# Gated linear attention and a GELU feed-forward on one core: the third unit's decay logits are loaded ahead of w_in, w_in comes in pieces of 512, 1024 and 512 columns, and the planner's priorities are drawn anew

## The chip, the cores and the metric

One core of a Trainium2 chip runs the whole program. The metric is the device time in microseconds (us). The kernel before takes 182.77 us (median of three runs, 182.22 to 183.18). The profiled execution has a span of 181.1 us from its first to its last recorded instruction, in a run of 183.18 us.

## What is computed

```python
def _attn_ref(q, k, v, f_logit):            # each 4 x 8 heads x 768 steps x 48
    f = 1.0 / (1.0 + np.exp(-f_logit))
    state = 0                                # per head 48 x 48
    for t in range(S):
        state = f[t][:, None] * state + outer(k[t], v[t])
        y[t] = q[t] @ state
x = y with the heads side by side            # 3072 tokens x 384
h = x @ w_in                                 # 384 x 2048
out = (0.5 * h * (1 + erf(h / sqrt(2)))) @ w_out     # 2048 x 384
```

The recurrence is computed in chunks of 128 steps. Inside a chunk it becomes matrix products of keys and queries that are scaled by exponentials of summed log decays; a 48 x 48 state per head is carried from chunk to chunk.

## The kernel before, in words

**Units and groups.** The 3072 tokens are 24 chunks of 128. Two chunks make a unit (12 units, numbered from 0); each unit's tokens are also one group of the feed-forward. Units 0 to 4 are "pair" units: each of their inputs comes in one transfer of 384 KB (line 449). Later units load each chunk by itself (line 457, 192 KB).

**Names of the operations** (given in the code as `name=`; the number behind is that of the unit, chunk or group):
- E and L (ScalarE, lines 494 and 497): exponential and logarithm of a unit's logits `fl`, 0.84 us each. C (TensorE, lines 526 and 515): sums of the log decays. RG, GT, GL (ScalarE, lines 543, 549, 570): exponentials of the sums. In units 2 to 4 the second chunk's sums come from G, a subtraction on VectorE (line 535).
- KP and QP (VectorE, for chunks 2 and 3 one each on GpSimd, line 576): keys and queries times these exponentials. VC (line 583): values cast to bf16, on GpSimd except in unit 1.
- Tk and Tq (TensorE, line 611): transposes of KP and QP in units 0 to 3; KQ (line 617) moves them to `kq`. From unit 4 on the transposes are DMAs (line 599).
- A (TensorE, line 784 in pair units): scores; AM (VectorE, line 631): masked scores. S (line 806): the chunk's contribution to the state; R, T, SB (VectorE line 655, GpSimd lines 657 and 662): the carried state. YI and YX (lines 826 and 705): outputs from the scores and from the state. YB (line 675), XT (line 691) and X (line 694): the outputs, transposed, as the group's input `xT`.
- F1 (TensorE, line 875): eight blocks per group, named F1.group.block, six matmuls each: `xT` times 256 columns of `w_in`. Blocks 0 and 1 take theirs from the first 512 columns of `w_in`, blocks 2 and 3 from the next 512, and so on. GE (ScalarE, line 885): the exact GELU of one block. F2 (line 896): four blocks of four matmuls per chunk, block r with piece r of `w_out`. O and st: eviction and store.

GE needs another activation table than E, L, RG, GT and GL; a change of table is a load of 1.28 us on ScalarE (line 953). F1 and F2 have four PSUM banks between them, so a fifth F1 waits for the GELU of the first.

**The order.** [...] That order is made when the program is built, by a planner (`Plan.run`, line 116): it places the ready operation with the earliest start by assumed durations, and breaks ties by a priority. To the priorities of each stretch of 20 it adds random numbers, whose seeds and spread stand in `SEEDS` (line 28). Where the planner sees TensorE idle in the first 30 us it inserts junk matmuls (line 947) that keep the engine busy.

**The transfers.** `LOADS` (line 238) lists them in order: `f0` is the logits of unit 0, `k`, `v`, `q` its keys, values and queries, `i` a piece of `w_in` and `o` a piece of `w_out`. The inputs go out from SyncE on the hardware DMA queue (q1 in the profile). The weights must be cast from f32 to bf16, so GpSimd issues them on the software queue (q0), in GpSimd's own program order, between its arithmetic. Both queues run on the same 16 DMA engines. The planner treats them as one chain, one transfer after another. On the chip only this much of the chain is kept, by `load` (line 382): a transfer whose predecessor in the list is on the other queue waits for one earlier transfer of that other queue.

```python
gate = None
if i and order[i - 1][0] != eng:
    back = 4 if eng == "pool" else 2
    for j in range(i - back, -1, -1):
        if order[j][0] != eng:
            gate = order[j][1]
            break
```

Before, this gives: `i0` waits for `f1`; `k2` waits for nothing of the other queue; `i1` waits for `k2`; `i2` and the pieces of `w_out` follow `i1` without a wait; `f3` waits for `o3`.

## Time and profile before

| | busy us | share of the span |
|---|---|---|
| TensorE matmul | 171.7 | 95% |
| of it junk matmuls (line 947, 36 of them) | 10.4 | 6% |
| ScalarE | 125.2 | 69% |
| VectorE | 96.3 | 53% |
| GpSimd | 53.6 | 30% |

A busy TensorE is not the same as a useful one: the junk matmuls are all in the first 28 us and stand for waiting. The part of the profile to read for this change is therefore the opening, in which the engine waits for inputs and weights. The stretches of the trace (busy time in windows), the answer on DMA (packets of each queue in a window) and the chain of waits show it. "To landing" of a transfer is the time from the start of its issue to its completion.

### The profile page before, as it was taken

How to read it: one execution, taken by the hardware profiler on the slowest of the kernel's cores; microseconds unless marked ns; L12 is line 12 of the kernel's file. 1: busy time of each engine (PE TensorE's matmuls, PEld its weight loads, DVE VectorE, ACT ScalarE, POOL GpSimd, SP SyncE). 2: the span in 40 equal slices, each digit the busy share in tenths (PEclk: the TensorE clock that was granted, in tenths of full speed). 3: DMA queues.
4: the chain of work that ended last, by engine and by line, in shares of the span. 5: the costliest groups of instructions: out<-in, count | busy, mean ns of one | idle time of the engine just before them, and what ended most of it. 6: DMA issues, size and time to landing. Idle time of an engine off the chain costs nothing.

```text
span 181.1 us, 4916 instructions
## 1 busy us (share of the span) xinstructions
PE 171.7 (95%) x1990; PEld 132.3 (73%) x1990; DVE 96.3 (53%) x194; ACT 125.2 (69%) x212; POOL 53.6 (30%) x116
## 2 busy tenths in 40 slices
PE   7788889999999999988999999999999999999993
PEld 2356669966787688785779689976697986886972
DVE  5289750058898564244896692527691625362110
ACT  2775198963899189999967759777585578560720
POOL 7657870003043641140176113112435110300000
PEclk9999999999999999999999999999999999999999
DMA  6999999949997898999999999999999872814102
GB/s 148 261 261 226 268 170 203 200 115 267 278 266 142 186 197 170 249 227 171 216 179 213 215 175 207 195 187 189 185 245 181 181 162 47 166 37 91 43 0 87
DMA packets 106998, 32.61 MB, mean 180 GB/s; under 512 B 102113, under 2 KB 106081, under 8 KB 106977
## 3 DMA queue, kind: packets, MB, share of 16 engines
q1 hardware_dynamic: 105056, 29.07, 79.7%
q0 software_dynamic: 1776, 3.15, 9.8%
q8 instruction: 15, 0.25, 0.6%
q10 hardware_dynamic: 144, 0.10, 0.2%
q14 instruction: 7, 0.05, 0.1%
HBM read 25.17 MB, written 4.72 MB: 165 GB/s over the span
## 4 chain that ended last, share of the span: by engine, by line
PE 64%; ACT 15%; DMA 15%; SPq 3%; issue 1%; DVE 0%; DVEq 0%
PE ps L875 26%; PE ps L896 25%; ACT gT L885 7%; DMA fl<-in_f_logit_dram 7%; DMA win<-in_moe_w_in_dram 5%; ACT L953 4%; SPq L449 3%; DMA kq<-sc 2%; PE ps L722 2%; PE ps L758 2%; PE ps L917 1%; ACT gt L549 1%; PE ps L521 1%; PE ps L699 1%; PE ps L745 1%
## 5 line engine op out<-in xcount | busy, mean ns | idle before, releaser
L885 ACT ACTIVATE gT<-ps 128x512 bf16<-128x512 f32 x96 | 57.5, 671 | 24.6 <-PE ps L875 23.0
L875 PE MATMUL ps<-xT,win 128*128 128x256 bf16 x576 | 68.7, 273 | 1.3 <-ACT gT L885 0.9
L896 PE MATMUL ps<-wout,gT 128*128 128x384 bf16 x368 | 66.0, 326 | 0.0
L875 PEld LDWEIGHTS <-win 128*128 128x128 bf16 x576 | 61.6, 114 | 3.9 <-issue 1.2
L896 PEld LDWEIGHTS <-gT 128*128 128x128 bf16 x368 | 34.2, 98 | 19.5
L583 POOL CAST vb<-vt 128x384 bf16<-128x384 f32 x22 | 12.6, 584 | 52.5 <-DMA vt<-in_v_dram 52.4
L631 DVE TENSOR_TENSOR am<-ps,mask 128x512 bf16<-128x512 f32 x28 | 17.6, 684 | 15.1 <-PE ps L722 15.1
L901 DVE COPY osb<-ps 128x384 f32<-128x384 f32 x20 | 11.1, 556 | 25.9 <-PE ps L896 18.2
L657 POOL TENSOR_TENSOR tn<-rr,gl 128x384 f32<-128x384 f32 x16 | 14.0, 872 | 35.2 <-DVE rr L655 34.6
L576 DVE TENSOR_TENSOR sc<-qt,gt 128x384 bf16<-128x384 f32 x23 | 14.0, 616 | 13.7 <-ACT gt L549 13.7
L576 DVE TENSOR_TENSOR sc<-kt,rg 128x384 bf16<-128x384 f32 x23 | 13.5, 597 | 11.3 <-ACT rg L543 11.3
L953 ACT ACT_TABLE_LOAD x15 | 19.2, 1283 | 0.3
L662 POOL CAST sb<-tn 48x192 bf16<-48x192 f32 x40 | 14.8, 371 | 11.6 <-DVE tn L651 6.6
L494 ACT ACTIVATE fl<-fl 128x768 f32<-128x768 f32 x12 | 10.1, 842 | 10.5 <-DMA fl<-in_f_logit_dram 10.5
L675 DVE CAST yb<-ps 128x384 bf16<-128x384 f32 x22 | 11.9, 555 | 7.4 <-PE ps L758 3.7
L631 DVE TENSOR_TENSOR am<-ps,maskp 128x512 bf16<-128x512 f32 x20 | 12.5, 684 | 2.2 <-PE ps L784 1.4
L543 ACT ACTIVATE rg<-ps 128x384 f32<-128x384 f32 x21 | 10.3, 503 | 4.4 <-PE ps L523 2.8
L549 ACT ACTIVATE gt<-ps 128x384 f32<-128x384 f32 x21 | 10.2, 503 | 3.9 <-PE ps L523 3.3
L947 PE MATMUL ps<-junk 128*128 128x512 bf16 (+3 forms) x36 | 10.4, 423 | 2.1 <-POOL junk L939 1.3
L655 DVE TENSOR_TENSOR rr<-ps,tn 128x384 f32<-128x384 f32 x16 | 8.9, 553 | 3.5 <-POOL tn L657 1.8
L497 ACT ACTIVATE lf<-fl 128x768 bf16<-128x768 f32 x12 | 10.1, 843 | 0.4
L947 PEld LDWEIGHTS <-junk 128*128 128x128 bf16 x36 | 3.6, 111 | 6.2 <-issue 3.5
(74 smaller groups left out, 130.4 us busy)
## 6 DMA issues: line engine op xcount, KB each, us to landing
out_dram<-osb SPq DMA_DIRECT2D x19, 192.0 KB, 3.1
fl<-in_f_logit_dram SPq DMA_DIRECT2D x14, 192.0 KB, 3.8
kt<-in_k_dram SPq DMA_DIRECT2D x14, 192.0 KB, 3.8
qt<-in_q_dram SPq DMA_DIRECT2D x14, 192.0 KB, 3.7
vt<-in_v_dram SPq DMA_DIRECT2D x14, 192.0 KB, 3.9
fl<-in_f_logit_dram SPq DMA_DIRECT2D x5, 384.0 KB, 6.2
kt<-in_k_dram SPq DMA_DIRECT2D x5, 384.0 KB, 6.2
vt<-in_v_dram SPq DMA_DIRECT2D x5, 384.0 KB, 5.7
```

What stands on the lines that cost most here:

```text
L549: P.add("ACT", 0.40, lambda g=gps[j], gtv=gtv: nc.scalar.activation(gtv(), g.t()[:, 0:HD].rearrange("q (p h d) -> q p h d", h=2, d=D), AF. ...
L576: P.add("POOL" if pl else "DVE", 0.80 if pl else 0.475, lambda a=a, y=y, j=j, w=w, pl=pl, b=(gtv if w else rg): (nc.gpsimd if pl else nc.v ...
L583: P.add("ACT" if hv else "POOL", 0.40 if hv else 0.47, lambda y=y, j=j, hv=hv: (nc.scalar.copy if hv else nc.gpsimd.tensor_copy)(y["vb"].t ...
L631: P.add("POOL" if pl else "DVE", 1.15 if pl else 0.61, lambda hh=hh, pl=pl: (nc.gpsimd if pl else nc.vector).tensor_tensor(ams[hh].t(), ap ...
L657: P.add("POOL", 0.83, lambda: nc.gpsimd.tensor_tensor(tn.t(), rr.t(), glb(), ALU.mult), rd=[("rr", n), ("gl", n)], wr=[("tn", n)], bufs=[r ...
L662: P.add("POOL", 0.36, lambda hh=hh: nc.gpsimd.tensor_copy(sb.t()[64 * hh:64 * hh + D, :, D * hh:D * hh + D], tn.t()[64 * hh:64 * hh + D, : ...
L675: P.add("ACT" if help_ else "DVE", 0.40 if help_ else 0.475, lambda: copier(help_)(yb.t()[:, i, :], yp.t()[:, 0:HD]), rd=[("yp", n)], wr=[ ...
L875: nc.tensor.matmul(hps.t()[:, i * tok:(i + 1) * tok].rearrange("a (s t) -> a s t", s=s), col(fo)[:, kk, :], xT.t()[:, :, kk, :], start=(kk ...
L885: nc.scalar.activation(to, fr, AF.Gelu)
L896: nc.tensor.matmul(op.t()[:, 0:d_model], gT.t()[:, fo, s_ * C:(s_ + 1) * C], wout[fo // 4][:, fo % 4, :], start=(fo == 0), stop=(fo == FO ...
L947: nc.tensor.matmul(o.opens.t()[:, 0:w], junk[:, 0:C], junk[:, 0:w], start=True, stop=True, skip_group_check=True)
L953: nc.scalar.preload_act_table_set({"exp": "natural_log_exp_and_others", "gelu": "gelu_and_others"}[o.table])
```

## The change

It does three things. The logits of unit 2 (`f2`) are loaded before the first pieces of `w_in`, so that ScalarE can do that unit's exponentials early, before its first change to the GELU table. The first piece of `w_in` is made smaller, so that the first F1 blocks can start on less data, and the larger second piece follows it at once. The first unit's queries move ahead of its keys and values. The random priorities of nine of the twelve stretches are drawn with other seeds, which makes another order on every engine.

```diff
-SEEDS = [1643, 41, 3215, 1275, 2533, 2502, 823, 887, 1264, 763, 2447, 3095]
+SEEDS = [1131, 1014, 2287, 2045, 3867, 2749, 2245, 1296, 1264, 763, 2447, 126]
...
-WIN = [1024, 512, 512]
+WIN = [512, 1024, 512]
...
-LOADS = ['f0', 'k0', 'v0', 'q0', 'f1', 'v1', 'k1', 'q1', 'i0', 'k2', 'f2', 'v2', 'q2', 'i1', 'i2', 'i3', 'o0', 'o1', 'o3', 'o2', 'f3', 'k3', 'q3', 'u4', 'v3']
+LOADS = ['f0', 'q0', 'k0', 'v0', 'f1', 'v1', 'k1', 'q1', 'f2', 'i0', 'i1', 'k2', 'v2', 'q2', 'i2', 'i3', 'o0', 'o1', 'o3', 'o2', 'f3', 'k3', 'q3', 'u4', 'v3']
```

(`i3` names no piece and loads nothing.) In the built program the rule of `load` now gives other waits: `i0` waits for `v1`; `i1` follows it without one; `k2` waits for `i0`; `i2` waits for `f2`; `o0` and `o1` follow `i2` without a wait; `f3` waits for `o3` as before.

The order of the built program around the opening, on TensorE: A1, F1.0.0, C of unit 2, F1.0.1, YI1, YX of unit 1, XT, F1.0.2, XT, F1.0.3, F1.0.4, Tk of chunk 4, F1, Tk of chunk 5, F1, S2, F1, Tq of chunk 4, F1, Tq of chunk 5, two F1, A2. Before it was: A1, three F1, YI1, YX, F1, XT twice, C of unit 2, twelve F1, six F2, and only then Tk and Tq of chunk 4. There are 25 junk matmuls instead of 36; no other instruction of TensorE is added or removed.

On GpSimd: VC twice, one SB, `i0`, `i1`, the second SB, KP2, T, SB twice, QP3, T, `i2`, `o0`, `o1`, SB twice, T, SB twice, VC of unit 2 twice, T, `o3`, SB twice, `o2`. On ScalarE the exponentials RG, GT and GL of unit 2 now stand before the first GELU, where before they stood behind the sixteenth.

## The prediction

> **What bounds the kernel now.** First the busy times and the slices of the page.

> ```profile
> PE 171.7 (95%) x1990; PEld 132.3 (73%) x1990; DVE 96.3 (53%) x194; ACT 125.2 (69%) x212; POOL 53.6 (30%) x116
> ...
> DMA  6999999949997898999999999999999872814102
> ```

> TensorE sets the end. Of its 171.7 us, 10.4 are junk, so 161.3 are useful. The timeline of TensorE shows it without a gap worth naming after 27.35 (0.44 at 55.05, 0.45 at 79.20, 0.4 at 84.14, some 1.5 us in all), and 3.0 us follow its end at 178.1. Useful work before 27.35 is therefore 161.3 - (150.75 - 1.5) = 12.0 us: 15.3 us of the opening are lost, and only there can much be won. The second line shows the DMA engines full in just that time.

> The chain of waits, in order of time, says what the opening waits for:

> ```profile
> 4.38 6.17 DMA fl<-in_f_logit_dram
> ...
> 10.84 9.78 DMA win<-in_moe_w_in_dram
> ...
> 20.67 2.16 PE ps L875 x18
> ...
> 26.38 1.13 PE ps L947 x5
> 27.52 1.32 PE ps L875 x12
> ```

> F1 starts at 20.67, when `i0` lands; junk at 26.38 waits for the first GELU, which stands behind E and L of unit 2. Their logits are late (ScalarE's timeline, idle 3.89 us before E):

> ```profile
> 22.56 0.84 ACT L494 ACTIVATE fl<-fl 128x768 f32<-128x768 f32 x1 [3.89 <-DMA fl<-in_f_logit_dram]
> ```

> Now the DMA answer (packets, MB, share of 16 engines), one us at a time. From 13 to 14 us, before `w_in` flows:

> ```profile
> q1 hardware_dynamic: 684, 0.26, 128.5%
> ```

> From 15 to 16 us, while `i0` flows:

> ```profile
> q0 software_dynamic: 86, 0.18, 92.5%
> q1 hardware_dynamic: 87, 0.03, 19.0%
> ```

> This is the line that decides. The two queues get packet for packet. A packet of `w_in` is 2 KB, one of the inputs 384 bytes, so the inputs fall from 684 packets a us to 87. It lasts from 14.5 to 19.1; `k2`, issued at 10.32, takes 10.7 us instead of the 6.2 of its forerunners.

> [...]

> **The change, part by part.**

> *Queries first, junk, seeds.* QP0 can start at 7.3 instead of 7.75; the four multiplies then end 0.4 us earlier, and A0 comes 0.7 earlier. This gain ends in the wait for `w_in` and is worth nothing. Eleven junk matmuls less cost and win nothing: they ran in waits. The seeds permute the same work; after 27.35 they can win at most the 1.5 us of gaps. I take 0, with -1 to +1.

> *`f2` earlier.* The first eight loads are through at about 14.0 (8,259 packets of 1,024 a load). `f2` is ninth now: done at 14.0 + 957/690 = 15.4, landing at about 16.5 instead of 22.5. E and L follow KQ on ScalarE (until 18.3) and end at 20.0. Five exponentials (0.37 each, GL 0.1) and G follow, then the table load, so the first GELU runs at about 25, 0.6 earlier.

> *`i0` smaller, but behind `v1`.* `v1` lands at 5.87 + 6.2 = 12.1; `i0` is issued at 12.2 instead of 10.84. From issue to first data took 3.7 us for `i0` (full queue) and 2.4 for `i1` (23.7 - 21.33). I take 3.7: data from 15.9, after `f2`. 384 packets at the 150 a us of 25 to 26 us take 2.5; completion 1.4 later, as before (19.2 to 20.63). It lands at 19.8 (18.5 to 20.5). F1.0.0 starts behind A1 at 19.9: 0.8 earlier. `i1` flows next, 384 packets at about 86: until 22.7, landing 24.3.

> *`k2` behind `i0`.* The new wait. Queued behind it on SyncE are `v2` and `q2`, and for these KP4, KP5, QP4, QP5, VC and, in order on TensorE, everything from Tk4 on. Issue at 19.8, first data 1.5 later, as with `f3` (issued 37.75; 548 packets by 40 at 690 a us): 21.3. The software queue then holds 125 packets of `i1`, 384 of `i2` and 128 each of `o0` and `o1` (393 KB at 3 KB), which GpSimd has issued by about 21: `i2` waits only for `f2`, not for `k2`. Before, `i1` waited for `k2` (21.0) and flowed from 23.7; in the gap `f2`, `v2` and `q2` came at full rate. Now there is no gap. Packet for packet, 765 software packets pass before most of `k2`'s 1,024: 125/86 = 1.4 us, 384/113 = 3.4 (113 is the rate of 24 to 25 us), and 0.79 MB at the 0.21 MB a us of 30 to 34, stretched by 15% = 4.3. Sum 9.1: at 30.4 `k2` has 260 packets left, 0.4 us more. It lands at 31.9, `v2` and `q2` 1.5 us apart at 33.4 and 34.9.

> *TensorE with this.* F1.0.0 to 20.6, C2 to 21.1, F1.0.1 to 21.7; YI1 waits for VectorE (QP3 on GpSimd ends at about 18.1 and Tq at 18.35; then KQ 0.68, R 0.55 and four AM of 0.62: 22.1), YX to 23.3; YB to 24.4; F1.0.2 with `i1` at 24.5, three F1 and two XT (0.655 and 0.17 each): 26.8. There it stands at Tk4, with one F1 (0.655) more done than the kernel before at 27.35: a lead of 27.35 + 0.65 - 26.8 = 1.2 us. KP4 takes 0.55 after `k2`: Tk4 at 32.5. The wait costs 5.7; S2 waits 0.2 for VC (0.95 after `v2`), Tq5 0.2 for QP5. Net 5.7 + 0.4 - 1.2 = **4.9 us**.

> *After that.* `o3` stands on GpSimd behind VC of unit 2, so it is issued at about 36.5 instead of 25.4. Alone it needs 2.4 + 2.0 + 1.4: 42.3. `f3` waits for it:

> ```profile
> SPq L449 <- DMA wout<-in_moe_w_out_dram: 16.8, 1, 16.8
> ```

> That wait ended at 37.75 before; 4.6 us later now, in step with TensorE, which has F1 and F2 of two groups to do. No further cost, and nothing catches up later with TensorE full. 182.8 + 4.9 = 187.7.

> **The rivals.**

> *Faster: inputs and weights don't hinder each other much.* Then `k2` lands at 21.3 + 1.5 + 1.1 = 23.9, `q2` at 26.9; no wait at Tk4, and the lead of 1.2 stays: 181.6. For it: the 7.1 MB in question would be through by 29.5 at 261 GB/s. Against it: 87 packets against 684, four us long.

> *Equal time instead of equal packets.* 3.0 us a load: `k2` 25.4, `v2` 28.4, `q2` 31.4. S2 waits 1.2 us, Tq4 1.4: 182.8 + 2.6 - 1.2 = 184.2. Against it, the shares of 92.5 and 19.0%.

> *The clock falls as well.* [...] Against it: part of that work waits for `q2` anyway.

> *`i0` flows early* (2.4 us after issue, at 14.6) and catches `f2`, which then lands at about 23. C2 blocks TensorE till 24.8, but SyncE's `k2` runs in the gap, since `i2` waits for `f2`; `q2` is again the last, at 35. About 187.5, with the stall elsewhere.

> **How the numbers follow.** Main case and early `i0`, which end alike: 0.55. Half clock 0.20. Equal time 0.10. Faster 0.15, of which 0.03 for a lead eaten by new gaps (no change); 0.02 of the equal-time case falls there too. So faster 0.12, same 0.05, slower 0.83. The range takes the main case with the seeds' 1 us and `i0`'s landing, equal time at its lower end and half clock at its upper: 184.0 to 190.0. It leaves out the faster case.

> **What would show it.** `f2` landing near 16.5 and F1 at 19.9 show the first steps right. The packets of q1 between 22 and 30 us, about 60 to 110 a us beside q0, and `k2` landing near 32, show the decisive one; TensorE must be idle from about 27 to 32 before line 611, then `f3` must go out near 42. If `k2` lands before 27, the forecast is wrong. After 60 us the traces should run in parallel.

## The result, and the profile after

The changed kernel takes 187.43 us (median of four runs, 186.54 to 188.09) against 182.5 for the kernel before on the same chip: a ratio of 1.026 (95% interval 1.021 to 1.031), 4.9 us more. The profiled execution spans 184.7 us, in a run of 186.54; before, it was 181.1, in a run of 183.18. So the two traces are only 3.6 us apart: one is of the fastest of four executions, the other of the slowest of four. What makes up the other 1.3 us of the 4.9 stands in no trace. In three of the experiments below, one execution of four took over 1.5% longer than the fastest; the ratios leave it out, the medians do not.

The page's row of TensorE, its granted clock and the DMA engines in 40 slices of 4.6 us:

```profile
PE 174.6 (95%) x1979; PEld 132.4 (72%) x1979; DVE 100.1 (54%) x194; ACT 126.4 (68%) x212; POOL 53.8 (29%) x116
...
PEclk9999589999999999999999999999999999999999
DMA  6999998199993999998989989979999793926102
```

The granted clock before:

```profile
PEclk9999999999999999999999999999999999999999
```

The junk is less (8.9 us instead of 10.4) and the engine is busier by 2.9. Part of that is the clock, which is halved from 17.6 to 24.4 us (mostly in the fifth and sixth slices); it was full before. The DMA row has a new hole, in the slice from 32 us on.

The longest pieces of the chain of waits from 5 to 36 us (start, length, what):

```profile
5.69 6.31 DMA vt<-in_v_dram
12.30 6.85 DMA win<-in_moe_w_in_dram
20.20 12.56 DMA qt<-in_q_dram
34.73 1.31 PE ps L875 x12
```

No E, no GELU and no `w_in` of 1024 columns ends last any more. `v1` releases `i0`, `i0` releases the inputs of unit 2, and the last of these, `q2`, takes 12.6 us. It then stops VectorE (QP4), and QP4 stops TensorE (Tq of chunk 4): from A1 to this Tq (20.85 to 33.40 us) TensorE starts its operations in the order in which the program was built. The timelines of VectorE and of TensorE:

```profile
32.78 0.56 DVE L576 TENSOR_TENSOR sc<-qt,gt 128x384 bf16<-128x384 f32 x1 [3.16 <-DMA qt<-in_q_dram]
```

```profile
20.85 1.07 PE L784 MATMUL ps<-kq 64*64 64x128 bf16 x32
21.85 0.29 PE L947 MATMUL ps<-junk 128*128 128x128 bf16 x1
21.93 1.49 PE L875 MATMUL ps<-xT,win 128*128 128x256 bf16 x6
...
28.89 0.82 PE L875 MATMUL ps<-xT,win 128*128 128x256 bf16 x6 [0.56 <-ACT gT L885]
29.54 0.39 PE L611 MATMUL ps<-ident,sc 128*128 128x128 bf16 x4
...
33.40 0.40 PE L611 MATMUL ps<-ident,sc 128*128 128x128 bf16 x4 [0.72 <-DVE sc L576]
```

A1 starts at 20.85 and the first F1 at 21.93, where the forecast has 19.9 for F1 and, by its sum, about 19.1 for A1. Tk4, which was to stand for 5.7 us, starts at 29.54 with no wait before it.

Why `q2` is slow, from the answers on DMA (packets, MB, share of 16 engines). From 22 to 23 us:

```profile
q1 hardware_dynamic: 732, 0.28, 107.0%
q0 software_dynamic: 4, 0.01, 3.4%
```

and from 27 to 28 us:

```profile
q0 software_dynamic: 77, 0.19, 99.2%
q1 hardware_dynamic: 73, 0.03, 14.9%
```

The inputs first have the engines to themselves. From 27 to 28 us they get one packet for each packet of the weights. Before that they get fewer still, from 25 to 26 us:

```profile
q0 software_dynamic: 154, 0.18, 111.9%
q1 hardware_dynamic: 9, 0.00, 2.0%
```

The issue of `q2` was over by then (20.20 to 22.89). Why the turns are not even in this stretch is not shown. So `k2` lands 5.2 us after its issue, `v2` 8.2, `q2` 12.6: at 24.4, 27.8 and 32.8.

A count by hand over TensorE's timeline shows what this means for useful work. The matmuls done up to a time t are added up, junk left out, each at its shortest back-to-back pitch (0.109 us for F1, 0.163 for F2, and so on). The table gives how far a kernel is behind the one before, in us of such work. It is good to about 0.3 us. The experiments are told below.

| at t | changed | weights held | held, KP2 and QP3 on VectorE |
|---|---|---|---|
| 28 us | 0.8 | 0.5 | -0.8 |
| 34 us | 2.8 | 0.9 | 0.3 |
| 66 us | 3.4 | 0.9 | -0.1 |
| 160 us | 3.8 | 1.8 | 1.2 |

Of the 3.8 us that are missing at 160, 2.8 are there at 34. In between the figure wanders (about 4.5 at 76 and 2.7 at 90), since the two kernels do their work in different orders.

### The profile page after: what moved, and what is told of

Same layout as the page of the kernel before. It is cut to its first block, busy times and chain, and to the rows that moved or that the text cites. A ratio compares the mean times of both kernels' runs of the same rounds, so it can differ in the third digit from the quotient of the medians.

```text
span 184.7 us, 4896 instructions
## 1 busy us (share of the span) xinstructions
PE 174.6 (95%) x1979; PEld 132.4 (72%) x1979; DVE 100.1 (54%) x194; ACT 126.4 (68%) x212; POOL 53.8 (29%) x116
## 4 chain that ended last, share of the span: by engine, by line
PE 72%; DMA 14%; DVE 5%; SPq 3%; issue 2%; ACT 2%; DVEq 0%; ACTq 0%
PE ps L896 31%; PE ps L875 29%; DMA qt<-in_q_dram 7%; DMA win<-in_moe_w_in_dram 4%; DMA vt<-in_v_dram 3%; SPq L449 3%; DVE sc L576 2%; PE ps L722 2%; PE ps L758 2%; PE ps L917 1%; PE ps L699 1%; PE ps L521 1%; DVE am L631 1%; PE ps L745 1%; ACT L953 1%
## 5 line engine op out<-in xcount | busy, mean ns | idle before, releaser
L885 ACT ACTIVATE gT<-ps 128x512 bf16<-128x512 f32 x96 | 58.1, 672 | 21.9 <-PE ps L875 20.2
L875 PE MATMUL ps<-xT,win 128*128 128x256 bf16 x576 | 71.0, 275 | 0.7 <-ACT gT L885 0.6
L896 PE MATMUL ps<-wout,gT 128*128 128x384 bf16 x368 | 66.7, 326 | 0.0
L875 PEld LDWEIGHTS <-win 128*128 128x128 bf16 x576 | 61.3, 114 | 3.5 <-issue 1.0
L631 DVE TENSOR_TENSOR am<-ps,mask 128x512 bf16<-128x512 f32 x28 | 17.6, 684 | 17.4 <-PE ps L722 17.4
L576 DVE TENSOR_TENSOR sc<-kt,rg 128x384 bf16<-128x384 f32 x23 | 15.7, 693 | 12.7 <-ACT rg L543 12.7
L662 POOL CAST sb<-tn 48x192 bf16<-48x192 f32 x40 | 15.6, 390 | 19.9 <-DVE tn L651 14.8
L576 DVE TENSOR_TENSOR sc<-qt,gt 128x384 bf16<-128x384 f32 x23 | 15.6, 683 | 9.1 <-ACT gt L549 5.9
L953 ACT ACT_TABLE_LOAD x15 | 19.2, 1283 | 0.3
L657 POOL TENSOR_TENSOR tn<-rr,gl 128x384 f32<-128x384 f32 x16 | 13.7, 858 | 12.6 <-DVE rr L655 10.2
L494 ACT ACTIVATE fl<-fl 128x768 f32<-128x768 f32 x12 | 10.2, 847 | 6.1 <-DMA fl<-in_f_logit_dram 6.0
L543 ACT ACTIVATE rg<-ps 128x384 f32<-128x384 f32 x21 | 10.4, 499 | 4.1 <-PE ps L523 3.7
L947 PE MATMUL ps<-junk 128*128 128x512 bf16 (+2 forms) x25 | 8.9, 498 | 1.3 <-POOL junk L939 1.3
L611 PE MATMUL ps<-ident,sc 128*128 128x128 bf16 x64 | 6.7, 235 | 3.5 <-DVE sc L576 2.7
```

What stands on the lines that cost most here:

```text
L543: P.add("ACT", 0.40, lambda g=gps[j], rg=rg: nc.scalar.activation(rg.t(), g.t()[:, 0:HD], AF.Exp, scale=-1.0), rd=[("g", n)], wr=[("rg", n ...
L576: P.add("POOL" if pl else "DVE", 0.80 if pl else 0.475, lambda a=a, y=y, j=j, w=w, pl=pl, b=(gtv if w else rg): (nc.gpsimd if pl else nc.v ...
L631: P.add("POOL" if pl else "DVE", 1.15 if pl else 0.61, lambda hh=hh, pl=pl: (nc.gpsimd if pl else nc.vector).tensor_tensor(ams[hh].t(), ap ...
L657: P.add("POOL", 0.83, lambda: nc.gpsimd.tensor_tensor(tn.t(), rr.t(), glb(), ALU.mult), rd=[("rr", n), ("gl", n)], wr=[("tn", n)], bufs=[r ...
L662: P.add("POOL", 0.36, lambda hh=hh: nc.gpsimd.tensor_copy(sb.t()[64 * hh:64 * hh + D, :, D * hh:D * hh + D], tn.t()[64 * hh:64 * hh + D, : ...
L875: nc.tensor.matmul(hps.t()[:, i * tok:(i + 1) * tok].rearrange("a (s t) -> a s t", s=s), col(fo)[:, kk, :], xT.t()[:, :, kk, :], start=(kk ...
```

## The experiments

Three things in the trace could each carry the loss: `q2` late, the clock halved, and VectorE late with A1. The first experiments take them apart. Each time is a median; the kernel before took 182.2 to 182.3 in their company.

**The clock: more junk in the changed kernel.** In the loop that inserts junk (ahead of line 947), three more matmuls of 512 columns before each of three operations:

```diff
+                room = {'Tk2': 12, 'S1': 12, 'Tk3': 12}.get(o.name, room)
```

> The kernel after, with three junk matmuls of 512 columns added before each of Tk of chunk 2, S1 and Tk of chunk 3 (all in waits between 14.8 and 18.6 us). Theory of the clock (too few matmuls from 14 to 19 us halve TensorE's clock from 17.4 to 24.6): the granted clock stays at full speed, A1 takes 0.57 us instead of 1.07 and an F1 0.66 instead of 1.3; 1.2 to 1.7 us faster, 185.9 +- 0.4. Theory that only transfers and VectorE hold the opening: the clock may stay up, but the time stays at 187.4 or rises by up to 0.3.

Measured: 187.86 us, ratio 1.029 (1.023 to 1.035). In the traced execution the clock is full in every slice (in two of the other three its mean is 0.991), and Tk4 starts at 28.14, 1.4 us earlier. VectorE's timeline shows where that goes:

```profile
32.69 0.56 DVE L576 TENSOR_TENSOR sc<-qt,gt 128x384 bf16<-128x384 f32 x1 [5.09 <-DMA qt<-in_q_dram]
```

The wait for `q2` grew from 3.16 to 5.09 and ends at the same time. The halved clock lies beside that wait and costs nothing as long as `q2` is late. In the run with T and SB moved, told below, two executions kept the full clock without more junk, and took 187.18 and 187.41 us.

**The weights: `i2`, `o0` and `o1` held back.** Their issues are moved in GpSimd's order behind VC of chunk 5, that is, until `v2` has landed:

```diff
+    def behind(names, last):
+        moved = [o for o in P.placed if o.name in names]
+        rest = [o for o in P.placed if o.name not in names]
+        at = max(i for i, o in enumerate(rest) if o.name == last) + 1
+        P.placed = rest[:at] + moved + rest[at:]
+    behind(['ii2', 'io0', 'io1'], 'VC5')
```

> The kernel after, with the issues of i2, o0 and o1 moved on GpSimd behind VC of unit 2, so that they wait for v2. Theory of the packets (q2 is held back to 32.8 us because the software queue is served packet for packet): q2 lands before 28.5, the wait of 0.7 us before Tq of chunk 4 is gone, 0.7 to 1.5 us faster, 186.3 +- 0.5. Theory that q2's delay is covered by a TensorE that is late anyway: 187.4 +- 0.4, with the same F1 and Tq times or another wait in their place.

Measured: 184.87 us, ratio 1.013 (1.008 to 1.019): half of the loss is gone. The answer on DMA from 23 to 24 us has the inputs alone:

```profile
q1 hardware_dynamic: 601, 0.23, 99.5%
```

and in VectorE's timeline QP4 waits for nothing:

```profile
28.17 0.55 DVE L576 TENSOR_TENSOR sc<-qt,gt 128x384 bf16<-128x384 f32 x1
```

`q2` lands at 27.3, and TensorE doesn't wait before Tq of chunk 4. So the 640 software packets that stood beside `v2` and `q2` cost about 2.5 us (2.6 by the medians, 2.2 by the ratios). The other half of the loss is not theirs. The move also takes 1.9 us of issues out of GpSimd's way: its last SB before VC ends at 23.25 instead of 24.71. What that adds is not separated, but with more junk an earlier TensorE won nothing while `q2` was late.

**The same in part: only `o0` and `o1` held**, with `i2` where it was (`behind(['io0', 'io1'], 'VC5')`).

> The changed kernel with only the issues of o0 and o1 moved on GpSimd behind VC of unit 2; i2 stays where it is. Theory of packets: 384 software packets instead of 640 stand beside v2 and q2, so q2 lands between the 27.3 us of the run with all three held and the 32.8 of the changed kernel, at about 29.2; TensorE reaches Tq of chunk 4 at 31.5 to 32 and does not wait there; 185.0 us (184.4 to 185.6). Rival, in which i2 alone does the harm: q2 near 32 and 187.4 us (186.8 to 188.0).

Measured: 185.5 us, ratio 1.017 (1.012 to 1.022); `q2` lands at 28.8. With 384 packets in the way `q2` and the time lie between the other two, though the time's interval overlaps that of the full hold.

**The other side: `k2` without its wait for `i0`.**

```diff
-            if gate is not None:
+            if gate is not None and name != "kt2":
```

> The kernel after, where k2 does not wait for i0. Theory of the packets (what holds q2 back is that i2, o0 and o1 follow i1 without a pause, not the wait of k2): k2 now shares packet for packet with i0 and i1 from 15.5 us, i1 is through at about 23.5 instead of 21 and i2 follows it at once, so the pause in the software queue from 21 to 23.5 is lost; q2 lands at 33.5 to 35 instead of 32.8 and the kernel is 1 to 2 us slower than after, 188.9 +- 0.7. Theory that the new wait of k2 for i0 is what costs: k2 lands before 20, q2 before 29, 185.5 +- 0.7.

Measured: 188.75 us, ratio 1.031 (1.024 to 1.038). `q2` goes out 4.1 us earlier, at 16.12, and lands at 33.1, 17 us later. From 20 to 21 us it shares with `i1`:

```profile
q0 software_dynamic: 87, 0.18, 93.5%
q1 hardware_dynamic: 86, 0.03, 18.8%
```

The wait for `i0` is therefore not what costs. With it or without, the inputs meet the weights packet for packet (86 and 87 here, 73 and 77 in the changed kernel from 27 to 28 us).

**VectorE: what GpSimd does meanwhile.** KP3 took 0.56 us on VectorE before, and 2.27 in the changed kernel. The lines before, of VectorE and of GpSimd:

```profile
15.26 0.56 DVE L576 TENSOR_TENSOR sc<-kt,rg 128x384 bf16<-128x384 f32 x1 [0.23 <-ACT rg L543]
15.27 1.40 POOL L576 TENSOR_TENSOR sc<-qt,gt 128x384 bf16<-128x384 f32 x1
```

and the timelines of both in the changed kernel:

```profile
14.30 2.27 DVE L576 TENSOR_TENSOR sc<-kt,rg 128x384 bf16<-128x384 f32 x1
16.50 0.55 DVE L675 CAST yb<-ps 128x384 bf16<-128x384 f32 x1
16.96 1.59 DVE L576 TENSOR_TENSOR sc<-qt,gt 128x384 bf16<-128x384 f32 x1
```

```profile
14.38 0.99 POOL L576 TENSOR_TENSOR sc<-kt,rg 128x384 bf16<-128x384 f32 x1
15.34 0.82 POOL L657 TENSOR_TENSOR tn<-rr,gl 128x384 f32<-128x384 f32 x1
16.22 0.96 POOL L662 CAST sb<-tn 48x192 bf16<-48x192 f32 x2
17.15 0.99 POOL L576 TENSOR_TENSOR sc<-qt,gt 128x384 bf16<-128x384 f32 x1
```

KP3 and QP2 each end 0.41 us after the last of GpSimd's multiplications beside them (16.16 and 18.14). The first try moved T and SB of GpSimd behind QP3, to shorten the run that KP3 waits out (`behind(['T1', 'SB1'], 'QP3')`).

> The kernel after, with T and SB of chunk 1 moved on GpSimd behind QP3, so that VectorE's KP3 meets less GpSimd work. Theory of the shared path (KP3 takes 2.27 us instead of 0.56 because VectorE and GpSimd hinder each other): KP3 ends before 15.9 instead of 16.6, QP3 earlier, A1 at about 19.5 instead of 20.85, 1.0 to 1.5 us faster, 186.2 +- 0.4. Theory that KP3 waits for its input k1 or RG and its length is only how the record shows it: A1 at 20.85 as before, 187.4 +- 0.4.

Measured: 187.29 us, ratio 1.025 (1.020 to 1.030). KP3 became longer:

```profile
14.53 3.22 DVE L576 TENSOR_TENSOR sc<-kt,rg 128x384 bf16<-128x384 f32 x1 [0.26 <-ACT rg L543]
```

GpSimd now does KP2, QP3 and T without a break, until 17.33, and KP3 ends 0.42 later. So the expected shortening failed, but the reading held: VectorE's multiplication again waited for a break in GpSimd's run. A1 came at 21.58, the time did not move: `q2` (32.5) covered this too.

**Hold and junk together.**

> The kernel after with i2, o0 and o1 held back as in e2_hold and the nine junk matmuls of e1_junk. Theory that q2 covered what the halved clock costs: now that q2 is early, the full clock shows, Tk of chunk 4 comes at about 28.1 instead of 28.5 us, 0.3 to 0.6 us faster than e2_hold, 184.4 +- 0.4. Theory that the clock costs nothing even then, because GELU and VectorE hold TensorE: 184.9 +- 0.3.

Measured: 184.5 us, ratio 1.012 (1.010 to 1.014). Not told apart from the hold alone; by the medians the clock costs 0.4 us then.

**Hold, and KP2 and QP3 on VectorE**, so that GpSimd has no run of multiplications there (line 576):

```diff
-(nc.gpsimd if pl else nc.vector).tensor_tensor(
+nc.vector.tensor_tensor(
```

> The changed kernel with i2, o0 and o1 held behind VC of unit 2, and with KP2 and QP3 done by VectorE instead of GpSimd. Theory that GpSimd's run of multiplications holds KP3 and QP2 on VectorE: KP3 takes about 0.56 us instead of 2.27 and A1 starts before 20.0 instead of at 20.85; with the inputs no longer late that time reaches the end: 183.9 us (183.4 to 184.4) against 184.9 with the hold alone. Rival, in which A1's lateness is covered by the wait for i0 and for the halved clock: A1 earlier, but 184.9 us (184.4 to 185.4).

Measured: 184.62 us, ratio 1.013 (1.009 to 1.017). A1 is as early as expected. The timelines of VectorE, TensorE and ScalarE:

```profile
14.07 1.96 DVE L576 TENSOR_TENSOR sc<-kt,rg 128x384 bf16<-128x384 f32 x2
```

```profile
19.16 0.46 PE L784 MATMUL ps<-kq 64*64 64x128 bf16 x17 [0.28 <-DVE kq L617]
```

```profile
25.73 4.35 ACT L885 ACTIVATE gT<-ps 128x512 bf16<-128x512 f32 x7
```

A1 starts at 19.16 and the first GELU at 25.73, and the clock stays full. KP3 did not come down to 0.56 us: of the 1.96 us, KP2 takes 0.55 and KP3 1.49, and KP3 ends at 16.02, again 0.41 us after a T of GpSimd (15.61). The gain in time failed: it is not resolved from the hold alone. Held back, `i2` is itself late here: TensorE waits 0.43 us for it at 32.60. As the table shows, this kernel has at most 0.2 us of useful work missing from 42 to 66 us, and still ends late: by 1.7 us between the spans of the two traces (182.8 and 181.1), by 2.4 in the medians. That loss comes afterwards. TensorE's busy time in windows (start and end, length, then the first busy time) is full in all but 0.94 us of these stretches before:

```profile
66.00:76.00 10.00, 10.00 (x127) 8.16 (x125) 2.20 (x6) 9.90 (x14) 1.51 (x3) 1.00 0.98 212
76.00:90.00 14.00, 13.06 (x137) 9.54 (x135) 8.03 (x16) 13.88 (x27) 2.64 (x5) 1.00 1.13 201
...
130.00:150.00 20.00, 20.00 (x219) 16.85 (x217) 10.51 (x19) 14.42 (x25) 4.98 (x9) 1.00 0.88 191
```

and in this experiment it lacks 0.51, 0.45 and 0.54:

```profile
66.00:76.00 10.00, 9.49 (x129) 8.59 (x128) 6.23 (x13) 9.45 (x17) 2.90 (x7) 1.00 1.05 181
76.00:90.00 14.00, 13.55 (x138) 9.78 (x137) 6.78 (x13) 13.59 (x21) 1.14 (x3) 1.00 1.00 201
...
130.00:150.00 20.00, 19.46 (x224) 16.41 (x222) 10.53 (x19) 13.65 (x25) 5.04 (x11) 1.00 0.88 190
```

Over all of 66 to 178 us TensorE is idle for 0.94 us before and for 1.84 here. So waits make up half of the 1.7 us. For the rest TensorE is busy longer over the same matmuls, and why is not shown.

**All three together.**

> The same with three more junk matmuls ahead of each of Tk2, S1 and Tk3, so that the clock stays full: theory that lateness of A1 and halved clock together are what the hold leaves of the loss in the opening: 183.5 us (183.0 to 184.0), and at 34 us no useful TensorE work less than before. Rival, in which what is left is lost later by the new order: 184.5 us (184.0 to 185.0), as with the hold and the junk.

Measured: 184.41 us, ratio 1.014 (1.009 to 1.019). By the median this is the rival, though the interval (183.9 to 185.7 us) just reaches the other theory. The opening is repaired (0.3 us behind at 34 us, level at 66 within the error of the count), and 2.2 us stay lost by the medians. But the traced execution, the fastest of five at 183.55, has a span only 0.7 us longer than the one before (181.8 against 181.1); the others took up to 186.03, and what they lose stands in no trace.

**The junk of the kernel before**, ten matmuls of it taken away (ahead of YI0, A1 and the first F1):

```diff
+                room = {'YI0': 0, 'A1.1': 0, 'A1.0': 0, 'F1.0.1': 0}.get(o.name, room)
```

> The kernel BEFORE, without its ten junk matmuls ahead of YI0, A1 and the first F1 (13.8 to 20.3 us). Theory of the clock: the granted clock falls to half between about 17 and 24 us, and the kernel becomes 0.8 to 1.7 us slower, 183.7 +- 0.4. Theory that junk in waits costs and wins nothing, as the prediction has it: 182.5 +- 0.3.

Measured: 182.68 us, ratio 1.0021 (1.0005 to 1.0036). In the traced execution the clock stayed full, with gaps of up to 1.17 us on TensorE. In four of the twelve its mean was 0.98 to 0.99, and these took 182.8 to 183.29 us; with the junk it was never below 0.997. So these junk matmuls are worth 0.4 us in that kernel, and part of it is that the clock falls in some executions without them.

**The seeds alone** (the kernel before with the new `SEEDS`) **and the loads alone** (the changed kernel with the old `SEEDS`):

> The kernel before with the new SEEDS alone (LOADS and WIN as before). Theory that the transfers make the change slower: 182.3 +- 1.0, the order of the seeds moves only the gaps after 30 us; its transfers land as before (q2 at about 25.7). Rival, that the new order makes it slower: 184 or more.

> The new LOADS and WIN with the old SEEDS. Theory of the packets: GpSimd again issues i2, o0 and o1 behind i1 without a pause, q2 lands at 32 us or later, 186.5 +- 1.0. Rival, that the new seeds make the change slower: 183 or less.

Measured: 192.95 us for the seeds, ratio 1.058 (1.055 to 1.060), and 199.69 for the loads, 1.092 (1.083 to 1.101). Both times lie far from what the theories expected. With the seeds alone the opening is as before, and TensorE waits from 90 us on; one such wait in its timeline, and the granted clock, which is halved twice for 3.4 us (from 100.6 and from 114.3):

```profile
98.62 0.34 PE L745 MATMUL ps<-vb,sc 128*128 128x96 bf16 x4 [1.38 <-DVE sc L576]
PEclk9999999999999999999996996999999999999999
```

With the loads alone the loss at 34 us is 3.5 us, much as with both, but on another path. Here GpSimd issues `i2` at 19.23, 1.2 us earlier, and the weights are back from about 22 us on. Now `k2` is the input that is caught: it lands at 29.4, and TensorE stands before Tk4:

```profile
30.03 0.40 PE L611 MATMUL ps<-ident,sc 128*128 128x128 bf16 x4 [2.61 <-DVE sc L576]
```

Some 10 us more are lost from 62 to 90 us. TensorE waits there, and the clock is halved from 69.1 to 82.8 us, which can cost at most half of that stretch, 6.8 us (its timeline, then the granted clock):

```profile
71.68 0.50 PE L521 MATMUL ps<-lf,trin 128*128 128x384 bf16 x1 [1.53 <-DVE am L631]
PEclk9999999999999955599999999999999999999999
```

The order after the opening is fitted to one list of loads. Neither part can be judged by itself.

## Why the forecast was right, and where its steps were not

The time was forecast at 187.7 us and came out at 187.43. The mechanism named is at work: inputs on the hardware queue, weights on the software queue, taken by turns packet by packet (73 and 77 from 27 to 28 us, though 9 and 154 from 25 to 26). The holds (2.5 and 1.9 us back) and the freed `k2` (no gain) show it. But it carries about half of the loss, where the forecast gave it a wait of 5.7 us, less a lead of 1.2. And by the forecast's own signs its path was wrong: `k2` landed before 27, and TensorE did not stand from 27 to 32 before Tk4. That the total still fits within 0.3 us is in good part luck: a term that was too large made up for losses on VectorE, by the clock and after the opening that its sum left out.

- **`f2` and `i0`.** `f2` landed at 17.5 (forecast 16.5). `i0` went out at 12.30 (12.2) and landed at 19.1 (19.8, range from 18.5). Right.
- **"Now there is no gap."** This is the step that failed. `i2` was issued at 20.39, close to the 21 assumed, but its data came only at 23.3, 2.9 us later: the forecast gave `i0` a delay of 3.7 us from issue to data, and gave `i2` none. Also `i1`, alone on the engines, moved 0.21 MB a us rather than 0.18, and was through at 21 instead of 22.7. In the pause from about 21 to 23.3 `k2` and most of `v2` came at full rate (672 and 732 packets a us). With the loads alone, where `i2` went out 1.2 us earlier, `k2` was caught as forecast and TensorE stood 2.6 us before Tk4.
- **Which input is caught.** Hence `k2` at 24.4 instead of 31.9, `v2` 27.8 instead of 33.4, and `q2` 32.8 instead of 34.9. Not Tk4 waits but Tq4, and the recorded wait is only 0.7 us instead of 5.7, since TensorE came later than forecast.
- **TensorE up to Tk4.** The forecast's sum has A1 at about 19.1 (Tq at 18.35, then KQ for 0.68) and the first GELU at about 25. It left out what GpSimd, with another T between KP2 and QP3, does to VectorE's multiplications. KP3 and QP2 took 2.27 and 1.59 us, A1 came 1.75 us late, and the first GELU at 28.09. With more junk and the clock full A1 came at 20.22, so some 0.6 us of this is the clock's. With KP2 and QP3 on VectorE, and the clock full, A1 and the first GELU came at 19.16 and 25.73, close to the forecast. The forecast's lead of 1.2 us at Tk4 was lost in these two ways; in that experiment there was a lead of 0.8 at 28 us.
- **The clock.** The forecast put a halved clock at 0.20, after the stall of 5.7 us. That was the author's estimate: in the trace of the kernel before the clock is full from 5.37 us to the end of its work, so it shows no fall after a wait. The fall came at 17.6 us, before any such stall, after a stretch in which TensorE was busy for 2.55 of 4 us (14 to 18). In the traces the clock was full where junk filled that stretch or where KP2 and QP3 were on VectorE (a mean of 1.000 each time). Its fall cost nothing beside `q2` (187.86 us with more junk, 187.43 without).
- **"Eleven junk matmuls less cost and win nothing."** Right within 0.4 us, by the two runs on junk. But the clock hung on it: without such junk it fell in some executions (a mean of 0.98 to 0.99 in four of twelve).
- **"The seeds permute the same work ... I take 0, with -1 to +1."** Too narrow in its idea. Taken alone the seeds cost 10.6 us. In the changed kernel, what they and the loads do after the opening costs 1.0 us (the count from 34 to 160 us); once the opening is repaired, it is 0.7 and 1.7 us in the traces and 2.2 to 2.4 in the medians. That this later loss comes from the new order, and not from a transfer or a later consequence of the hold, is argued from the windows; no run restores the old order there, so the cause stays open.
- **`o3` and `f3`.** `o3` went out at 34.91 (36.5), `f3` at 39.25 (42). They were earlier than forecast, and it is right that they cost nothing more: 2.95 us behind at 38 and 2.60 at 50.

Of the 4.9 us, then, about 2.5 are the weights beside `q2`, shown by the holds. Some 0.6 us (0.9 to 0.3 in the table at 34 us) hang on VectorE and the clock together, by the count only, since the times of the repaired versions aren't resolved from the hold's. The rest, between 1 and 2 us, is lost later or, as the two traces differ by only 3.6 us, from one execution to the next; its cause stays open. The terms overlap: while `q2` is late, neither of the others costs anything. No version measured here beats the kernel before.

## What to carry to other kernels

If weights and inputs share the DMA engines from two queues, let the large-packet queue wait for the last input that is needed sooner, not for the first of the list (here the 640 packets of weights beside `v2` and `q2` cost about 2.5 us); a wait that happens to stand between them is a protection that a new list removes. When several things are late side by side, repairing the one that ends first shows nothing, so begin with the one that ends last. An order fitted by random search belongs to its list of loads: change one, and the whole has to be measured.

## What the runs showed of the hardware that was not expected

**VectorE waited out GpSimd's multiplications.** In four places of three traces a VectorE product of two operands in SBUF that started during a run of GpSimd's instructions ended 0.41 to 0.42 us after the last product of the run (15.61 to 16.02, 16.16 to 16.57, 17.33 to 17.75, 18.14 to 18.55), whether the run had one product or three. Each time an instruction of GpSimd, a cast SB, was already under way when VectorE's product began: in the changed kernel from 14.07 to 14.41, with KP3 from 14.30, and from 16.84 to 17.18, with QP2 from 16.96. With two and three products in the run KP3 took 2.27 and 3.22 us instead of 0.56. It is not always so. Before, GpSimd's KP2 ended at 15.31 and QP3 followed without a break, and yet VectorE's KP3 came in between: it took 0.56 us from 15.26, and QP3, from 15.27, took 1.40 us instead of 0.99. What decides this is not shown.

**A piece of 1024 columns on the software queue was faster than one of 512.** Alone on the engines `i1` moved 0.20 to 0.22 MB a us. The prediction had read 150 packets of 1 KB (0.15) in the kernel before; pieces of 512 columns moved 0.15 to 0.19 almost alone (before, from 25 to 28 us).
